# Squared-ReLU attention with an MLP on one Trainium2 core: the first chunk's loads in another order, and v's high part rounded on ScalarE

## The chip, the cores and the metric

The kernel runs on one core of one Trainium2 chip (trn2). The metric is the device time of one execution in microseconds, the median of several runs. A measurement of this kernel can tell about 0.2% (4 us) from no change.

The engines are called as in the profile: PE (matmul), DVE (VectorE), ACT (ScalarE), POOL (GpSimd) and SP (SyncE, which issues most DMAs here). Each engine works through its own instructions in order, and so does each queue of DMA issues: whatever stands behind a waiting instruction waits too.

## The reference

```python
# batch 4, seq S = 3008, d_model 256, d_qk 64, d_ff 2048
scores = (1.0 / S) * np.matmul(z, z.transpose(0, 2, 1))
attn = np.maximum(scores, 0.0) ** 2
out = np.matmul(attn, v)
x = (u * out).reshape(B * S, D)
h = x @ w_in
g = h * np.clip(h + 3.0, 0.0, 6.0) / 6.0
return g @ w_out
```

w_in and w_out come in as 64-bit floats, the rest as 32-bit floats.

## The kernel before, in words

**Tiling.** Each batch has 6 chunks of 512 rows (the last has 448), so there are 24 chunks; in the trace chunks are counted from 0. A chunk is worked through in 12 pairs of two 128-row blocks of keys. For each pair `scores` makes s (four matmuls, z times z), relu and square, and `attend` adds the pair to o (twelve matmuls). The matmuls use a 32-bit format that rounds its operands. So every operand is kept as a high part, rounded, and a low part, the rest: vh and vl, ah and al, zx and zy (each holding a high and a low half), w_in_h and w_in_l. `split` (L75 to L78) makes the two: ACT copies to the high part, which rounds, and DVE subtracts. Each product takes three matmuls.

**Symmetry.** The scores are symmetric. Where block k of chunk c is needed as block c of chunk k later, the square r2 is stored to DRAM (tiles d, `keep`, L257 to L260), fetched again (tiles l, `fetch_pair`, L240, four DMAs a pair), transposed on DVE to rm (`turn`, L271) and split (`from_mirror`, L285, L287). At most two fetched pairs exist at a time; `fetch_mirrored` fetches the next ones, both from the main loop and at the end of each `turn`.

**Weights.** The 64-bit weights are taken apart on DVE in pieces of 128x512: `split64` and `finish64` make 8 DVE steps a piece (L101, L106, L110, L114, L119, L123, then L131, L133) and one ACT cast (L117). There are 16 pieces, in the order in which the MLP reads them: in 0, in 1, out 0, in 2, and so on to in 7, out 6, out 7. `weight_ops` is a generator, and `weight_work(n)` takes n steps of it; its first step issues the loads (wraw) of the first two pieces. wraw tiles come from the pool of tag "r" (5 buffers), the same that holds the relu rt, the square r2 and the transposed rm. `weight_needed` takes steps until the piece that a unit reads is ready.

**Order.** One program order is written by hand in the last part: a few calls ahead of the loop, and then, for each chunk i and pair p, `split_v` and `split_z` of the first batch, `scores` of a pair one or two ahead (two while g = 12 i + p is under FIRST = 28), `fetch_mirrored`, `turn_next`, fetches, `weight_work`, `attend`, and from g = 28 on the MLP units: `up` (h, twelve matmuls, L418, L419) and `down` (y, twelve matmuls), 1.4 a pair on average. Each engine's order follows from that.

**First batch.** z and v of batch 0 are loaded while chunk 0 is worked on. Ahead of the loop stand z 0, v 0, z 1, v 1, the first weight loads and then z 2, v 2, v 3. In the loop v 4 and later ones are fetched four pairs ahead, z 3 to z 5 at pairs 0, 2 and 4, each behind the stores of that pair. For batch 0 the high part of v is a second load of the same v by POOL's queue, which rounds on the way (`rounded=b == 0`), and so are the high parts of z for chunks from 2 on.

**Names.** zraw, vraw and wraw are loads as they arrive; t is scratch of the weights; u is the load of u, multiplied by o on DVE (L388); x is that product and xh, xl its split (L77, L78).

Of the kernel before, what the change touches and what calls it, by code (L numbers as in the profile page):

```python
# [13 lines left out]
B, S, D, DQK, DFF = 4, 3008, 256, 64, 2048  # L14
NT = B * S
P = 128
CH = 512
NCH = 6
NJ = 24
NPAIR = NJ // 2  # L20
# [10 lines left out]
def relu2_attention_then_hswish_mlp(  # L31
# [22 lines left out]
    nc = tc.nc  # L54
# [14 lines left out]
    def f(ap):  # L69
        return ap.bitcast(F32)  # L70
# [4 lines left out]
    def split(hi, lo, raw, rounded=False):  # L75
        if not rounded:
            nc.scalar.copy(out=hi, in_=raw)  # L77
        nc.vector.tensor_tensor(out=lo, in0=raw, in1=f(hi), op=ALU.subtract)  # L78
# [86 lines left out]
    def fetch_v(b, p):  # L165

        if b == 0 and p < NPAIR - 1:
            raw = vpool.tile([P, 2, D], F32, tag="vl", name="vraw")
        else:
            raw = stg.tile([P, 2, D], F32, tag="stg", name="vraw")  # L170
        vh = vpool.tile([P, 2, D], F32R, tag="vh", name="vh")
        vt[b, p] = vh
        raws["v", p] = raw
        j0 = p * 2 * P
        for dst, queue in ((raw, nc.sync), (vh, nc.gpsimd))[:1 if b else 2]:
            if p < NPAIR - 1:
                queue.dma_start(
                    out=dst, in_=v[b, j0:j0 + 2 * P, :].rearrange("(r q) d -> q r d", q=P)
                )
            else:  # L180
                queue.dma_start(out=dst[:, 0, :], in_=v[b, j0:j0 + P, :])
                for h in range(2):
                    queue.dma_start(out=dst[64 * h:64 * h + 64, 1, :], in_=v[b, j0 + P:S, :])

    def split_v(b, p):
        vh, raw = vt[b, p], raws.pop(("v", p))
        vl = vpool.tile([P, 2, D], F32R, tag="vl", name="vl")
        split(vh, vl, raw, rounded=b == 0)
        vt[b, p] = (vh, vl)

    def fetch_z(b, k):
        if b == 0:
            raw = xpool.tile([P, CH], F32, tag=("xh0", "xh1", "xl0", "xl1")[k % 4], name="zraw")
        else:
            raw = stg.tile([P, CH], F32, tag="stg", name="zraw")
        zx = zpool.tile([P, CH], F32R, tag="zx", name="zx")
        zy = zpool.tile([P, CH], F32R, tag="zy", name="zy")
        zt[b, k] = (zx, zy)
        raws["z", k] = raw
        cols = slice(k * CH, (k + 1) * CH)  # L200
        nc.sync.dma_start(out=raw, in_=zz[b, :, cols])
        if b == 0 and k > 1:
            nc.gpsimd.dma_start(out=zx[0:64], in_=zz[b, 0:64, cols])
            nc.gpsimd.dma_start(out=zy[64:128], in_=zz[b, 64:128, cols])
# [149 lines left out]
    def width(c):  # L354
        return CH if c < NCH - 1 else S - CH * (NCH - 1)
# [20 lines left out]
    def load_u(b, c):  # L376
        n = width(c)
        t0 = b * S + c * CH
        t = upool.tile([P, 2, CH], F32, tag="u", name="u")
        nc.sync.dma_start(  # L380
            out=t[:, :, :n], in_=ut[:, t0:t0 + n].rearrange("(k p) t -> p k t", p=P)
        )
        raw_x[b, c] = t
# [69 lines left out]
    chunks = [(b, c) for b in range(B) for c in range(NCH)]  # L453
# [63 lines left out]
    def weight_work(n):  # L517
        for _ in range(n):
            next(w_ops, None)
# [39 lines left out]
    with tc.manual_schedule():  # L559
        nc.vector.memset(three, 3.0)  # L560
        fetch_z(0, 0)
        fetch_v(0, 0)
        split_z(0, 0)
        fetch_z(0, 1)
        fetch_v(0, 1)
        weight_work(1)
        split_v(0, 0)
        split_z(0, 1)
        scores(0, 0, 0)
        fetch_z(0, 2)  # L570
        fetch_v(0, 2)
        scores(0, 0, 1)
        fetch_v(0, 3)
        g_done = 2
        to_fetch += [(b, c, p) for b, c, p in pairs if p // 2 < c]
        g_turned = [2]
        for i, (b, c) in enumerate(chunks):
            ahead = b + 1 if c == NCH - 1 and b + 1 < B else None
            for p in range(NPAIR):
                g = i * NPAIR + p  # L580
                lead = 2 if g < FIRST else 1
                if i == 0:
                    if p + 1 < NPAIR:
                        split_v(0, p + 1)
                    if p % 2 == 0 and p // 2 + 2 < NCH:
                        split_z(0, p // 2 + 2)
                early = lead == 2 and p == NPAIR - 1
                if early:
                    attend(b, c, p)
                while g_done < min(g + lead + 1, len(pairs)):  # L590
                    scores(*pairs[g_done], square_on_act=i < 3)
                    g_done += 1
                if p > 3:
                    fetch_mirrored()
                if p < NPAIR - 1 or early:
                    turn_next()
                if i == 0:
                    if p + 4 < NPAIR:
                        fetch_v(0, p + 4)
                    if p % 2 == 0 and p // 2 + 3 < NCH:  # L600
                        fetch_z(0, p // 2 + 3)
                    if p == 6:
                        load_u(*chunks[0])
                        load_u(*chunks[1])
                maybe_split()
                if g >= FIRST:
                    weight_work(5)
                elif p < NPAIR - 2:
                    weight_work(4 if i else 2)
                if ahead and p < NPAIR - 1:  # L610
                    if p:
                        split_v(ahead, p - 1)
                    if p < NPAIR - 2:
                        fetch_v(ahead, p)
                    if p % 2 == 1:
                        fetch_z(ahead, p // 2)
                    elif p:
                        split_z(ahead, p // 2 - 1)
                elif b and c == 0 and p < 4:
                    if p in (1, 2):  # L620
                        split_v(b, NPAIR - 3 + p)
                    if p < 2:
                        fetch_v(b, NPAIR - 2 + p)
                    if p == 2:
                        fetch_z(b, NCH - 1)
                    if p == 3:
                        split_z(b, NCH - 1)
                if not early:
                    attend(b, c, p)
                    turn_next()  # L630
                if p == NPAIR - 1:
                    avs[0] += 1
                total = len(pairs) - FIRST
                target = max(0, g + 1 - FIRST) * ((len(chunks) - 1) * NU - 4) // total
                mlp_units(target - units_done[0])
        mlp_units(1)
        maybe_split()
        mlp_units(len(chunks) * NU - units_done[0])
# [35 lines left out]
```

## Time and profile before

| | |
|---|---|
| median of 3 runs | 1997.01 us (1996.62 to 1998.65) |
| profiled execution, time | 1998.23 us |
| profiled execution, span | 1996.4 us |
| PE busy | 1959.4 us, 98%, 8688 matmuls |
| DVE busy | 1280.7 us, 64% |
| ACT busy | 987.5 us, 49% |
| DMA queues | 178.14 MB; SP's 34.3% of 16 engines' span, POOL's 0.9% |

The profile is of one execution. Busy time is the sum of the instructions of an engine; matmuls overlap, so a matmul lasts 0.39 us and the next one starts 0.227 us after it. The granted clock of PE is given as a share of its full speed: 1.00 is 2.4 GHz and 0.50 is 1.2 GHz. An "idle before" in a row of the timeline is how long the engine stood still ahead of that row, with what ended it; "issue" stands for a wait that the profile doesn't name.

### The profile page before, as it was taken

What the parts mean: (1) busy time and instruction counts of PE and PEld (TensorE: products, weight loads), DVE (VectorE), ACT (ScalarE), POOL (GpSimd) and SP (SyncE); (2) the same over time, 40 slices, a digit from 0 to 9 for tenths busy, and PEclk for the clock granted to TensorE, in tenths of its full rate; (3) what the DMA queues carried; (4) which work ended last, traced back from release to release, by engine and by line L of the source; (5) the groups of instructions that cost most, each with busy time, mean ns of one, the idle gap of its engine ahead of it and who ended that gap; (6) DMA issues with size and microseconds to landing.
All of it is one profiled execution on the core that took longest, in us unless ns stands there. A gap on an engine that the chain in (4) does not pass through costs nothing.

```text
span 1996.4 us, 22062 instructions
## 1 busy us (share of the span) xinstructions
PE 1959.4 (98%) x8688; PEld 1637.0 (82%) x8688; DVE 1280.7 (64%) x1277; ACT 987.5 (49%) x1057; POOL 14.2 (1%) x26
## 2 busy tenths in 40 slices
PE   7899999999999999999999999999999999999999
PEld 5677788788888888888888888888888888888888
DVE  5798765676556566577565665657756565666654
ACT  6665444455444444456544454444554544444343
POOL 2000000000000000000000000000000000000000
PEclk9899999999999999999999999999999999999999
DMA  9663233424323233253333232324342323332300
GB/s 266 201 160 103 64 82 72 115 71 116 82 64 81 72 74 95 50 128 89 95 82 90 55 93 53 101 62 109 90 116 61 86 59 92 74 82 60 94 10 20
DMA packets 403271, 178.14 MB, mean 89 GB/s; under 512 B 250080, under 2 KB 385248, under 8 KB 403168
## 3 DMA queue, kind: packets, MB, share of 16 engines
q1 hardware_dynamic: 399232, 172.55, 34.3%
q0 software_dynamic: 3936, 4.20, 0.9%
q8 instruction: 68, 1.11, 0.2%
q14 instruction: 35, 0.29, 0.1%
HBM read 104.07 MB, written 72.61 MB: 89 GB/s over the span
## 4 chain that ended last, share of the span: by engine, by line
PE 90%; DVE 4%; DMA 2%; ACT 2%; issue 1%; SPq 1%; DVEq 0%; ACTq 0%
PE o L73 34%; PE h L73 24%; PE y L73 24%; PE s L73 7%; DMA zraw<-in_zz_dram 1%; DVE rm L271 1%; DMA vraw<-in_v_dram 1%; DVE rt L419 1%; DVE al L287 1%; ACT rt L418 0%; ACT gh L77 0%; ACT rt L320 0%; SPq L240 0%; DVE gl L78 0%; DMA d<-r 0%
## 5 line engine op out<-in xcount | busy, mean ns | idle before, releaser
L419 DVE SCALAR_TENSOR_TENSOR rt<-rt,h 128x1024 f32<-128x1024 f32 (+1 forms) x192 | 230.0, 1198 | 420.6 <-ACT rt L418 420.4
L418 ACT ACTIVATE rt<-h,three 128x1024 f32<-128x1024 f32 (+1 forms) x192 | 211.0, 1099 | 550.2 <-PE h L73 544.4
L73 PE MATMUL o<-ah,vl 128*128 128x512 f32 (+1 forms) x1152 | 448.1, 389 | 13.3 <-DVE u L388 6.2
L73 PE MATMUL o<-ah,vh 128*128 128x512 f32 (+1 forms) x1152 | 446.8, 388 | 0.0
L73 PE MATMUL o<-al,vh 128*128 128x512 f32 (+1 forms) x1104 | 429.2, 389 | 3.5 <-DVE al L287 3.5
L73 PE MATMUL y<-gh,w_out_l 128*128 128x512 f32 (+1 forms) x768 | 296.3, 386 | 1.7 <-DVE w_out_l L133 1.7
L73 PE MATMUL y<-gl,w_out_h 128*128 128x512 f32 (+1 forms) x768 | 296.3, 386 | 1.1 <-DVE gl L78 1.1
L73 PE MATMUL y<-gh,w_out_h 128*128 128x512 f32 (+1 forms) x768 | 296.0, 385 | 0.0
L73 PE MATMUL h<-xh,w_in_l 128*128 128x512 f32 (+1 forms) x768 | 295.9, 385 | 0.0
L73 PE MATMUL h<-xl,w_in_h 128*128 128x512 f32 (+1 forms) x768 | 295.9, 385 | 0.0
L73 PE MATMUL h<-xh,w_in_h 128*128 128x512 f32 (+1 forms) x768 | 295.8, 385 | 0.0
L78 DVE TENSOR_TENSOR gl<-rt,gh 128x1024 fp32r<-128x1024 f32 (+1 forms) x192 | 230.7, 1202 | 80.5 <-ACT gh L77 77.9
L73 PEld LDWEIGHTS o<-ah,vl 128*128 128x128 f32 x1152 | 218.2, 189 | 60.6 <-issue 11.9
L77 ACT CAST gh<-rt 128x1024 fp32r<-128x1024 f32 (+1 forms) x192 | 197.2, 1027 | 122.8 <-DVE rt L419 122.8
L73 PEld LDWEIGHTS o<-ah,vh 128*128 128x128 f32 x1152 | 218.3, 189 | 40.9
L73 PEld LDWEIGHTS o<-al,vh 128*128 128x128 f32 x1104 | 209.0, 189 | 45.8 <-DVE al L287 5.7
L320 ACT ACTIVATE rt<-s 128x1024 f32<-128x1024 f32 x168 | 171.3, 1020 | 129.9 <-PE s L73 125.1
L332 DVE TENSOR_TENSOR r<-rt 128x1024 f32<-128x1024 f32 (+1 forms) x140 | 170.0, 1214 | 95.7 <-ACT rt L320 95.6
L340 DVE TENSOR_TENSOR al<-r,ah 128x1024 fp32r<-128x1024 f32 x140 | 171.0, 1221 | 22.3 <-ACT r L330 8.6
L73 PEld LDWEIGHTS y<-gh,w_out_l 128*128 128x128 f32 x768 | 144.2, 188 | 29.8 <-DVE w_out_l L133 1.3
L73 PEld LDWEIGHTS y<-gl,w_out_h 128*128 128x128 f32 x768 | 144.2, 188 | 28.9 <-DVE gl L78 2.1
L73 PEld LDWEIGHTS y<-gh,w_out_h 128*128 128x128 f32 x768 | 144.2, 188 | 27.1
(51 smaller groups left out, 1807.0 us busy)
## 6 DMA issues: line engine op xcount, KB each, us to landing
d<-r SPq DMA_DIRECT2D x220, 256.0 KB, 2.9
l<-d SPq DMA_DIRECT2D x320, 128.0 KB, 3.3
l<-d SPq DMA_DIRECT2D x160, 112.0 KB, 2.9
vraw<-in_v_dram SPq DMA_DIRECT2D x44, 256.0 KB, 3.3
u<-in_ut_dram SPq DMA_DIRECT2D x20, 512.0 KB, 4.2
out_dram<-y SPq DMA_DIRECT2D x40, 256.0 KB, 3.1
zraw<-in_zz_dram SPq DMA_DIRECT2D x24, 256.0 KB, 3.6
wraw<-in_w_in_dram SPq DMA_DIRECT2D x8, 512.0 KB, 4.5
```

What stands on the lines that cost most here:

```text
L73: nc.tensor.matmul(out, lhsT=lhsT, rhs=rhs, start=start, stop=stop)
L77: nc.scalar.copy(out=hi, in_=raw)
L78: nc.vector.tensor_tensor(out=lo, in0=raw, in1=f(hi), op=ALU.subtract)
L271: nc.vector.transpose(out=rn.rearrange("p r (k e) -> p r k e", e=32), in_=t[:, :n // 32].rearrange("p k (r e) -> p r k e", r=2),)
L287: nc.vector.tensor_tensor(out=al[:, :, :n], in0=rn, in1=f(ah[:, :, :n]), op=ALU.subtract)
L320: nc.scalar.activation(out=rn, in_=s[:, :, :n], func=AF.Relu, scale=1.0 / S)
L332: nc.vector.tensor_tensor(out=r2_of, in0=r_of, in1=r_of, op=ALU.mult)
L340: nc.vector.tensor_tensor(out=l_of, in0=r2_of, in1=h_of, op=ALU.subtract)
L418: nc.scalar.activation(out=rn, in_=h, func=AF.Relu, bias=three)
L419: nc.vector.scalar_tensor_tensor(out=rn, in0=rn, scalar=6.0, in1=h, op0=ALU.min, op1=ALU.mult)
```

## The change

Four things change, all of them in the order or the way in which data of the first batch and the weights come in.

- Ahead of the loop z 2, z 3, v 2 and v 3 are fetched before the first score, and the call that issues the first weight loads is gone. In chunk 0, v of four pairs ahead and z 4 and z 5 are fetched at the head of a pair, ahead of its scores and their stores.
- v's high part in batch 0 is made as in other batches, by ACT from the loaded raw tile; POOL's second load of v is gone.
- `fetch_mirrored` is called in the loop only from pair 7 on, where it was from pair 4, and the first two loads of u come at pair 7, where they came at pair 6.
- At pair 0 of every chunk ahead of FIRST no weight steps are taken, so the first weight loads are issued at pair 1 of chunk 0.

```diff
     def split_v(b, p):
         vh, raw = vt[b, p], raws.pop(("v", p))
         vl = vpool.tile([P, 2, D], F32R, tag="vl", name="vl")
-        split(vh, vl, raw, rounded=b == 0)
+        split(vh, vl, raw)
         vt[b, p] = (vh, vl)
...
         split_z(0, 0)
         fetch_z(0, 1)
         fetch_v(0, 1)
-        weight_work(1)
+        fetch_z(0, 2)
+        fetch_z(0, 3)
+        fetch_v(0, 2)
+        fetch_v(0, 3)
         split_v(0, 0)
         split_z(0, 1)
         scores(0, 0, 0)
-        fetch_z(0, 2)
-        fetch_v(0, 2)
         scores(0, 0, 1)
-        fetch_v(0, 3)
...
                 if i == 0:
+                    if p + 4 < NPAIR:
+                        fetch_v(0, p + 4)
+                    if p < 2:
+                        fetch_z(0, p + 4)
                     if p + 1 < NPAIR:
                         split_v(0, p + 1)
...
-                if p > 3:
+                if p > 6:
                     fetch_mirrored()
                 if p < NPAIR - 1 or early:
                     turn_next()
-                if i == 0:
-                    if p + 4 < NPAIR:
-                        fetch_v(0, p + 4)
-                    if p % 2 == 0 and p // 2 + 3 < NCH:
-                        fetch_z(0, p // 2 + 3)
-                    if p == 6:
-                        load_u(*chunks[0])
-                        load_u(*chunks[1])
+                if i == 0 and p == 7:
+                    load_u(*chunks[0])
+                    load_u(*chunks[1])
                 maybe_split()
                 if g >= FIRST:
                     weight_work(5)
-                elif p < NPAIR - 2:
+                elif 0 < p < NPAIR - 2:
                     weight_work(4 if i else 2)
```

In `fetch_v` the loop over two destinations and queues becomes the one load by SP.

**SP, start of chunk 0.** The queue of SP from its first load on; r_181 and r_190 are the square of pair 2, r_226 and r_232 that of pair 3. Before:

```order
L201 DMA zraw<-in_zz_dram 128x512
L177 DMA vraw<-in_v_dram 128x2x256
L201 DMA zraw<-in_zz_dram 128x512
L177 DMA vraw<-in_v_dram 128x2x256
L152 DMA wraw<-in_w_in_dram 128x2x512 x2
L201 DMA zraw<-in_zz_dram 128x512
L177 DMA vraw<-in_v_dram 128x2x256
L177 DMA vraw<-in_v_dram 128x2x256 [waits DMAHW0_49]
L257 DMA d_184<-r_181 512x1x128 [waits DMAHW1_49,Activation_49]
L257 DMA d_184<-r_181 512x1x128 [waits DMAHW2_49]
L177 DMA vraw<-in_v_dram 128x2x256 [waits DMAHW3_49]
L201 DMA zraw<-in_zz_dram 128x512 [waits DMAHW4_49]
```

Now, from the fifth load on (the first four are the same):

```order
L200 DMA zraw<-in_zz_dram 128x512 x2
L176 DMA vraw<-in_v_dram 128x2x256 x2
L176 DMA vraw<-in_v_dram 128x2x256 [waits DMAHW0_49]
L200 DMA zraw<-in_zz_dram 128x512 [waits DMAHW1_49,DVE_49]
L256 DMA d_193<-r_190 512x1x128 [waits DMAHW2_49,Activation_49]
L256 DMA d_193<-r_190 512x1x128 [waits DMAHW3_49]
L176 DMA vraw<-in_v_dram 128x2x256 [waits DMAHW4_49]
L200 DMA zraw<-in_zz_dram 128x512 [waits DMAHW5_49,DVE_49]
L256 DMA d_193<-r_232 512x1x128 [waits DMAHW6_49,Activation_49]
L256 DMA d_193<-r_232 512x1x128 [waits DMAHW7_49]
L152 DMA wraw<-in_w_in_dram 128x2x512 [waits DMAHW0_49,DVE_49]
L152 DMA wraw<-in_w_in_dram 128x2x512 [waits DMAHW1_49]
```

All of z but the last piece stands ahead of the first store now, and the two wraw loads have moved from ahead of the first store to behind the second.

**DVE, pairs 2 to 4 of chunk 0.** The same pairs on DVE, from the al of pair 2 to that of pair 4. Before:

```order
L340 TENSOR_TENSOR al<-r_181,ah 128x1024
L101 TENSOR_SCALAR t_198<-wraw 128x512
L106 SCALAR_TENSOR_TENSOR t_198<-wraw,t_198 128x512
L78 TENSOR_TENSOR vl<-vraw,vh 128x512
L340 TENSOR_TENSOR al<-r_226,ah 128x1024
L110 TENSOR_SCALAR wraw<-wraw 128x512
L114 SCALAR_TENSOR_TENSOR t_198<-wraw,t_198 128x512
L78 TENSOR_TENSOR vl<-vraw,vh 128x512
L78 TENSOR_TENSOR zy<-zraw,zx 64x512
L78 TENSOR_TENSOR zx<-zraw,zy 64x512
L340 TENSOR_TENSOR al<-r_263,ah 128x1024
```

Now:

```order
L339 TENSOR_TENSOR al<-r_190,ah 128x1024 [waits Activation_49]
L78 TENSOR_TENSOR vl<-vraw,vh 128x512 [waits DMAHW6_49,Activation_49]
L339 TENSOR_TENSOR al<-r_232,ah 128x1024 [waits Activation_49]
L101 TENSOR_SCALAR t_242<-wraw 128x512 [waits DMAHW0_49]
L78 TENSOR_TENSOR vl<-vraw,vh 128x512 [waits DMAHW7_49,Activation_49]
L78 TENSOR_TENSOR zy<-zraw,zx 64x512 [waits DMAHW5_49,DMASW2_49]
L78 TENSOR_TENSOR zx<-zraw,zy 64x512 [waits DMASW3_49]
L339 TENSOR_TENSOR al<-r_273,ah 128x1024 [waits PE_49,Activation_49]
```

The first weight step, which waits for its load, stands behind the al of pair 3 and ahead of its vl; it stood a pair earlier.

**DVE, pairs 0 to 2 of chunk 3.** t_1423 and t_1504 are the scratch of the piece in 7, t_1490 and t_1623 that of out 6; the rt is that of the unit that reads in 7. Before:

```order
L131 TENSOR_TENSOR t_1423<-t_1423,w_in_h 128x512
L133 TENSOR_TENSOR w_in_l<-t_1423,w_in_l 128x2x256 [waits DVE_49]
...
L131 TENSOR_TENSOR t_1490<-t_1490,w_out_h 128x512
L133 TENSOR_TENSOR w_out_l<-t_1490,w_out_l 128x512 [waits DVE_49]
L419 SCALAR_TENSOR_TENSOR rt<-rt,h 128x1024 [waits Activation_49]
L78 TENSOR_TENSOR gl<-rt,gh 128x1024 [waits Activation_49]
L287 TENSOR_TENSOR al<-rm,ah 128x1024 [waits Activation_49]
L271 STREAM_TRANSPOSE rm<-l 128x1024 [waits DMAHW2_49,DMAHW7_49,DMAHW1_49,DMAHW0_49]
```

Now:

```order
L131 TENSOR_TENSOR t_1504<-t_1504,w_in_h 128x512
L133 TENSOR_TENSOR w_in_l<-t_1504,w_in_l 128x2x256 [waits DVE_49]
L101 TENSOR_SCALAR t_1657<-wraw 128x512 [waits DMAHW2_49]
L418 SCALAR_TENSOR_TENSOR rt<-rt,h 128x1024 [waits Activation_49]
L78 TENSOR_TENSOR gl<-rt,gh 128x1024 [waits Activation_49]
L286 TENSOR_TENSOR al<-rm,ah 128x1024 [waits Activation_49]
L270 STREAM_TRANSPOSE rm<-l 128x1024 [waits DMAHW6_49,DMAHW7_49,DMAHW1_49,DMAHW0_49]
...
L131 TENSOR_TENSOR t_1623<-t_1623,w_out_h 128x512
L133 TENSOR_TENSOR w_out_l<-t_1623,w_out_l 128x512 [waits DVE_49]
```

The last step of out 6 stood directly ahead of that rt, and stands 12 rows behind it now; the last step of in 7 stands two rows ahead of it, where it stood 13.

## Rows read from the trace of the kernel before

**Rows 1.** The table of stretches (from and to in us, length, then busy time and number of instructions of PE, weight loads, DVE, ACT and POOL, the granted clock of PE, the share of the DMA engines, GB/s).

```profile
0.00:71.10 71.10, 51.86 (x180) 39.48 (x180) 44.28 (x62) 40.82 (x43) 14.23 (x26) 0.88 0.99 258
32.90:38.20 5.30, 5.27 (x13) 4.14 (x14) 3.10 (x5) 5.01 (x6) 0.00 (x0) 0.50 0.51 148
53.90:62.20 8.30, 7.10 (x16) 5.16 (x17) 8.20 (x12) 3.60 (x4) 0.00 (x0) 0.50 1.05 340
72.40:75.90 3.50, 3.50 (x10) 2.77 (x9) 2.79 (x4) 1.04 (x1) 0.00 (x0) 0.52 0.55 110
400.00:1996.00 1596.00, 1589.74 (x7128) 1336.55 (x7126) 994.45 (x938) 773.35 (x829) 0.00 (x0) 1.00 0.31 78
```

**Rows 2.** What PE waited for over the whole span (us in total, times, the longest).

```profile
PE s L73 <- DVE zx L78: 7.1, 2, 6.2
PE s L73 <- issue: 6.9, 2, 4.5
...
PE y L73 <- DVE w_out_l L133: 1.7, 2, 0.9
```

**Rows 3.** The timeline of PE in chunk 0 and where chunk 1 begins (start, duration, operation, idle time before it).

```profile
24.70 0.39 PE L73 MATMUL o<-ah,vl 128*128 128x512 f32 x1
...
29.96 0.47 PE L73 MATMUL s<-zy,zx 128*128 128x512 f32 x1 [2.38 <-issue]
...
41.96 0.39 PE L73 MATMUL s<-zy,zx 128*128 128x512 f32 x1
...
45.58 0.39 PE L73 MATMUL s<-zy,zx 128*128 128x512 f32 x1
...
53.92 0.77 PE L73 MATMUL s<-zy,zx 128*128 128x512 f32 x1 [4.55 <-issue]
...
63.07 0.39 PE L73 MATMUL s<-zx 128*128 128x512 f32 x1
...
71.14 0.47 PE L73 MATMUL o<-ah,vl 128*128 128x512 f32 x1 [2.21 <-DVE vl L78]
```

**Rows 4.** The timelines of SP's queue (start, time of issue, number of issues), of DVE and of ACT in chunk 0.

```profile
18.55 0.63 SPq L201 DMA_DIRECT2D zraw<-in_zz_dram  x1
20.75 1.32 SPq L257 DMA_DIRECT2D d<-r  x2
...
39.26 7.31 SPq L240 DMA_DIRECT2D l<-d  x8
...
47.33 0.47 SPq L201 DMA_DIRECT2D zraw<-in_zz_dram  x1
...
28.46 0.68 DVE L78 TENSOR_TENSOR zy<-zraw,zx 64x512 fp32r<-64x512 f32 x1 [4.81 <-DMA zraw<-in_zz_dram]
...
52.41 0.68 DVE L78 TENSOR_TENSOR zy<-zraw,zx 64x512 fp32r<-64x512 f32 x1 [6.98 <-DMA zraw<-in_zz_dram]
...
19.68 1.04 ACT L330 ACTIVATE r<-rt 128x1024 f32<-128x1024 f32 x1
```

**Rows 5.** The DMA view of three short stretches: the loads of weights issued at 2.6 to 3.7 us, at 53.7 to 54.4 and at 87.9 to 88.6, with their size and the median time to landing in us.

```profile
wraw<-in_w_in_dram SPq DMA_DIRECT2D x2, 512.0 KB, 11.0
...
wraw<-in_w_in_dram SPq DMA_DIRECT2D x1, 512.0 KB, 6.7
...
wraw<-in_w_in_dram SPq DMA_DIRECT2D x1, 512.0 KB, 4.2
```

**Rows 6.** Groups of ACT's instructions from 0 to 74 us, shapes kept apart (count, busy us, mean ns of one, idle time before them and what ended it).

```profile
L320 ACT ACTIVATE rt<-s 128x1024 f32<-128x1024 f32 x12 | 12.3, 1024 | 13.9 <-PE s L73 9.7 <-DMA d<-r 3.8 <-DVE al L340 0.2
L329 ACT ACTIVATE ah<-rt 128x1024 fp32r<-128x1024 f32 x10 | 10.6, 1062 | 0.3
L330 ACT ACTIVATE r<-rt 128x1024 f32<-128x1024 f32 x10 | 10.4, 1045 | 7.8 <-DMA d<-r 7.8
...
L117 ACT CAST w_in_h<-t 128x512 fp32r<-128x512 f32 x2 | 1.2, 598 | 0.0
```

**Rows 7.** The timeline of DVE at the end of chunk 2 and the start of chunk 3.

```profile
181.59 0.69 DVE L344 TENSOR_TENSOR al<-r,ah 128x512 fp32r<-128x512 f32 x1 [1.00 <-ACT r L330]
...
184.20 1.24 DVE L271 STREAM_TRANSPOSE rm<-l 128x1024 f32<-128x1024 f32 x1
185.36 0.39 DVE L119 TENSOR_SCALAR wraw<-t 128x512 uint32<-128x512 uint32 x1
...
188.05 1.22 DVE L287 TENSOR_TENSOR al<-rm,ah 128x1024 fp32r<-128x1024 f32 x1
...
201.56 0.42 DVE L101 TENSOR_SCALAR t<-wraw 128x512 uint32<-128x512 uint32 x1
...
203.08 1.21 DVE L419 SCALAR_TENSOR_TENSOR rt<-rt,h 128x1024 f32<-128x1024 f32 x1
...
207.72 0.65 DVE L114 SCALAR_TENSOR_TENSOR t<-wraw,t 128x512 f32<-128x512 f32 x1
...
210.80 1.21 DVE L419 SCALAR_TENSOR_TENSOR rt<-rt,h 128x1024 f32<-128x1024 f32 x1
...
217.74 0.69 DVE L131 TENSOR_TENSOR t<-t,w_out_h 128x512 f32<-128x512 f32 x1
```

**Rows 8.** The timeline of PE in the same place: the first h of the unit that reads in 7, and the first y of the units that read out 6 and out 7.

```profile
204.59 0.39 PE L73 MATMUL h<-xh,w_in_l 128*128 128x512 f32 x1
...
211.03 0.47 PE L73 MATMUL y<-gh,w_out_l 128*128 128x512 f32 x1 [0.84 <-DVE w_out_l L133]
...
219.20 0.50 PE L73 MATMUL y<-gh,w_out_l 128*128 128x512 f32 x1 [0.89 <-DVE w_out_l L133]
```

More of the change, by code (lines that the diff above doesn't have):

```diff
@@ L174, in fetch_v @@
         j0 = p * 2 * P
[L175 to L183, printed above, removed]
+        if p < NPAIR - 1:
+            nc.sync.dma_start(
+                out=raw, in_=v[b, j0:j0 + 2 * P, :].rearrange("(r q) d -> q r d", q=P)
+            )
+        else:
+            nc.sync.dma_start(out=raw[:, 0, :], in_=v[b, j0:j0 + P, :])
+            for h in range(2):
+                nc.sync.dma_start(out=raw[64 * h:64 * h + 64, 1, :], in_=v[b, j0 + P:S, :])
     def split_v(b, p):
```

## The prediction

> **What bounds the kernel now.** The table of engines comes first: PE is busy 98% of the span, so only the places where PE stands still or runs at its lower clock can be won or lost. The table by stretches says where these are: from 400 us on, PE works 1589.7 of 1596.0 us, all at 1.00; in the first 71.1 us it works only 51.9 us, with a mean granted clock of 0.88 [rows 1]. PE's waits name the causes: s behind the split of z (7.1 us, 6.2 of it the start), s behind "issue" twice (6.9 us in all), and later y behind a weight, w_out_l, 1.7 us [rows 2]. The timeline of PE puts places to them: 2.38 us before the s at 29.96, 4.55 before that at 53.92, 2.21 before the o at 71.14 [rows 3]. For the first two the rows of DVE and SP tell what "issue" hides: DVE waited for zraw until 28.46 and 52.41, and SP had issued those two loads only at 18.55 and 47.33, behind stores, the second also behind 7.31 us of mirrored fetches [rows 4]. A stall costs twice, since the granted clock is lower afterwards: after the second, 8.3 us at 0.50 [rows 1]. In steady state a pair costs PE 3.62 us (the s at 41.96 and at 45.58, 16 matmuls apart, 0.227 each) [rows 3].
>
> So I treat two stages apart: chunk 0, whose loads the change reorders, and the start of the fourth chunk (index 3), some 200 us in, where the weights are first needed and where DVE is the engine that PE waits for.
>
> **Part 1, z and v earlier, chunk 0.** In the new order z2 and z3 and v2 and v3 leave SP before any store, z4 behind them, z5 behind the first store. The waits of DVE for zraw (4.81 and 6.98 us) [rows 4] go, and with them the PE stalls at 29.96 and 53.92.
>
> What is late next is a weight. Before, the two first wraw loads were issued among the first loads and took 11.0 us to land [rows 5], while DVE asked for one only after 18 us. Now they stand in SP's queue behind the store of pair 3, and DVE's order has the first weight step between the al of pair 3 and vl of pair 3. Everything on DVE queues behind that wait. The square that this store writes out starts at 19.68 and takes 1.04, and its two issues start at 20.75 and take 1.32, so the first wraw leaves at 22.1 [rows 4]. Landing took 4.2 us on a quiet queue, 6.7 behind other 512 KB loads, 11.0 in the crowd at the start [rows 5]; here two of them go out together beside one store, and I take 5.5, near the lower two: 27.6. One weight step (0.58, below), vl (0.68, as the split of z [rows 4]) and 0.14 to PE give 29.0 for the o of pair 3, which started at 24.70 before [rows 3]: a new stall of 4.3 us, in place of those removed. Behind it I set one stretch at the low clock, of 2.3 us (13 matmuls in 5.27 us against 2.95 at 0.227 each [rows 1]).
>
> From there PE has six pairs of 3.62 to the end of the last s of the chunk, 21.7 us. From that end (63.07 + 0.23) to the o at 71.14 there were 7.84 us: square, al, transposes, weight steps and vl in DVE's order, which the change leaves as it is [rows 3]. Sum: 4.3 + 2.3 + 21.7 + 7.8 = 36.1 us against 46.4 (24.70 to 71.14): **10.3 us won**. The ends: a landing of 4.2 and no clock stretch give 13.9; a landing of 11.0 gives 4.8.
>
> **Part 2, v rounded on ScalarE.** Twelve loads of v by POOL go. ACT gets 12 casts of 128x512, and the same form on weights took 0.598 us [rows 6], so 7.2 us in chunk 0. Its three passes per pair are 1.02 + 1.06 + 1.05 us [rows 6]; with 0.60 that is 3.7 against PE's 3.62. Casts that stand between pairs thus cost 0 to 0.1 per pair, at most 1.5 us with the weight casts; ACT had 7.8 us of waits for stores of r2 [rows 6], which should become fewer, as wraw takes two of the five r buffers later. I take 0 for both together, and keep 1.5 for the end of the range.
>
> **Part 3, mirrored fetches at p > 6.** The 7.31 us of issues [rows 4] move from pair 4 to pair 7, ahead of the u loads, one weight load and the stores of the last two pairs. Their first transposes come behind the al of the last pair, two pairs (7.2 us) and a square later; the issues end by then. Cover gone would be a wait of 1 us; I take 0.
>
> **Part 4, weights later, which the diff shows in one line.** `elif 0 < p < NPAIR - 2` leaves out the weight steps of pair 0 of every chunk ahead of FIRST: 2 in chunk 0, 4 in chunk 1, 4 in chunk 2, and the call before the loop goes too. DVE is 11 steps behind the old order when the MLP starts, and 5 per pair don't catch up: the order now has the last weights forced in directly ahead of the units that read them. Until the end of chunk 2 each weight still stands well ahead of its unit. In chunk 3 it does not.
>
> I count from the first transpose at the end of chunk 2, at 184.20. There DVE had just waited 1.00 us for ACT, so it cannot have been earlier, and it is not later now [rows 7]. The old order ended w_in's last piece at 201.56, and its h started at 204.59, unhindered [rows 7, 8]. Five weight steps took 2.69 us (185.36 to 188.05) and 3.08 us (207.72 to 210.80) [rows 7], 0.577 each. The new order has 11 steps more ahead of that piece (6.35 us), and also rt, al, gl and a transpose, which stood behind it (203.08 to 207.72, 4.64 us): 201.56 + 6.35 + 4.64 = 212.55. With 0.14 to PE, h can't start before 212.7, 8.1 us later than it did.
>
> Then a chain without overlap. h takes 12 matmuls, 2.72. ACT's relu takes 1.1 with its hop. From rt to behind xl DVE took 210.80 to 217.74, 6.94 us [rows 7], and its order now has those ahead of the rest of the next-to-last w_out piece: 7 steps, 4.04. With 0.14 to PE: 14.9 us, so the y that started at 211.03 starts at 227.6. The last y follows behind another y and o, 5.44 us, at 233.1, where it was 219.20 [rows 8]: **13.9 us lost**. PE stands still for about 8 and 9 us on this way, both longer than the 4.55 that brought the low clock before [rows 1, 3]; I add 2.3 us for each, 4.6. The ends: no such stretch, 13.9; two like that of 53.9 to 62.2 (16 matmuls in 7.10 us against 3.63, 3.5 lost [rows 1]), 20.9.
>
> A rule on that last term. The rows show three stretches at about half clock, with 1.2 to 3.5 us lost in each [rows 1], every one behind a stall of over 2 us [rows 3]. The Trainium skill, in "TensorE: Matmul & The Clock Gate", section "What's actually happening", holds that for modelling "the ramp penalty is <1% of a typical kernel span" and should not be fitted to a count. Without the three new stretches (2.3 + 4.6) the sum would be 1998.3 and not 2005.2: true as a share, and yet all the distance from no change to slower.
>
> **Sum.** -10.3 + 0 + 0 + 13.9 + 4.6 = +8.2 us. The profiled execution took 1998.23 us, its span 1996.4 with 1.8 around it; that is 1.2 above the median of 1997.01, so the profile of the changed kernel should show about 2006.4 and the median 2005.2. The ends of the parts give +0.0 (13.9 won, 13.9 lost) to +17.6 (3.3 won, 20.9 lost).
>
> **Rivals.**
> - *The two sides cancel.* The wraw loads land in 4.2 us, no low clock follows, and the losses in chunk 3 stay near 13.9 to 17: 1997 to 2000. For it: 2.21 us of standstill cost only 1.2 us afterwards [rows 1, 3]. Against: the two long stalls are far longer. Chance 0.17.
> - *The weights don't bind, faster.* The late weights are caught in DVE's slack, and only chunk 0 counts: 1997.0 - 10.3 = 1986.7. For it: y waited for weights only 1.7 us so far [rows 2], so the old order had some room. It decides whether DVE ends w_in's last piece by 204.45; by the order it would have to do 11 steps and four other operations 8 us faster. Chance 0.13.
> - *The early loads don't help, slower still.* The weight loads are as slow as at the start (11.0), and chunk 0 wins 4.8 or less; the change then only swaps zraw for wraw as what DVE waits for. 1997.0 - 4.8 + 18.5 = 2010.7. For it: the same two loads took 11.0 [rows 5]. Against: POOL's loads of v are gone then. Chance 0.08.
>
> **How the numbers follow.** The forecast has the other 0.62: 2005.2, by itself 2001 to 2013. What a measurement can tell from no change is 0.2%, 4.0 us: 1993.0 to 2001.0. The forecast and the third rival are slower: 0.70; the first is the same: 0.17; the second is faster: 0.13. A range from 1994 to 2013 leaves out the second rival and a few hundredths at the top.
>
> **What would show it.** Right: no DVE wait for zraw after 20 us; one for wraw at its first step on weights, near 22 to 28; the chunk's last o on a new pair starting near 61 instead of 71.1; then, ten microseconds earlier than in the old rows, y and h behind L133 for several microseconds twice, near 195 to 220, with a granted clock under 1 there. Wrong: PE without gaps over 2 us between 180 and 240, or the last pair of chunk 0 later than 67.

## The result and the profile after

The changed kernel takes 2020.90 us (median of 4 runs, 2018.25 to 2023.20), the kernel before beside it 1996.82 us. The ratio is 1.0116, 95% interval 1.0103 to 1.0128: slower, as forecast, but by 24 us where 8 were forecast, and outside the range. The profiled execution of the changed kernel has a span of 2021.4 us, 25.0 more than before.

The timeline of PE, with the starts that answer to [rows 3] and [rows 8], and the start of chunk 1's pairs:

```profile
28.53 0.79 PE L73 MATMUL o<-ah,vl 128*128 128x512 f32 x1 [3.94 <-DVE vl L78]
...
68.08 0.80 PE L73 MATMUL o<-ah,vl 128*128 128x512 f32 x1 [8.51 <-DVE vl L78]
...
96.48 0.50 PE L73 MATMUL o<-al,vh 128*128 128x512 f32 x1 [0.98 <-DVE al L339]
...
105.22 0.50 PE L73 MATMUL o<-al,vh 128*128 128x512 f32 x1 [1.19 <-DVE al L339]
...
113.96 0.50 PE L73 MATMUL o<-al,vh 128*128 128x512 f32 x1 [1.70 <-DVE al L339]
...
124.00 0.77 PE L73 MATMUL o<-ah,vl 128*128 128x512 f32 x1 [4.70 <-DVE u L387]
...
197.25 0.47 PE L73 MATMUL o<-ah,vl 128*128 128x512 f32 x1 [1.68 <-DVE u L387]
...
207.74 0.50 PE L73 MATMUL y<-gh,w_out_l 128*128 128x512 f32 x1 [1.46 <-DVE w_out_l L133]
...
217.19 0.77 PE L73 MATMUL h<-xh,w_in_l 128*128 128x512 f32 x1 [6.40 <-DVE w_in_l L133]
...
235.35 0.76 PE L73 MATMUL y<-gh,w_out_l 128*128 128x512 f32 x1 [9.96 <-DVE w_out_l L133]
...
242.88 0.39 PE L73 MATMUL y<-gh,w_out_l 128*128 128x512 f32 x1
```

Two of them in the kernel before:

```profile
120.27 0.69 PE L73 MATMUL o<-ah,vl 128*128 128x512 f32 x1 [3.70 <-DVE u L388]
...
192.99 0.47 PE L73 MATMUL o<-ah,vl 128*128 128x512 f32 x1 [1.49 <-DVE u L388]
```

Read as a ledger, each row against the same matmul before (PE's order is the same in both kernels). The last o of chunk 0, that is the first matmul that adds its last pair: 68.08 for 71.14, **3.1 us won**. The first o behind chunk 1, at 124.00, was at 120.27: 3.7 behind, so **chunk 1 lost 6.8**. Then come the weights: the y at 235.35, which reads out 6, was at 211.03, 24.3 behind; the o at 197.25 was at 192.99 and had been 4.3 behind, so **20.1 were lost there** and 0.5 on the way. The rest of the span adds 0.7: -3.1 + 6.8 + 0.5 + 20.1 + 0.7 = 25.0.

The table of stretches (columns as in [rows 1]) shows that behind 240 us next to nothing is lost:

```profile
190.00:220.00 30.00, 20.15 (x80) 15.32 (x79) 25.72 (x36) 8.69 (x10) 0.00 (x0) 0.93 0.47 105
220.00:240.00 20.00, 10.04 (x31) 7.68 (x30) 13.51 (x17) 5.71 (x7) 0.00 (x0) 0.68 0.30 62
240.00:2021.00 1781.00, 1772.00 (x7928) 1488.65 (x7926) 1104.39 (x1040) 855.98 (x917) 0.00 (x0) 1.00 0.32 78
```

Where chunk 0's gain went is read from DVE and SP (columns as in [rows 4]) and from the DMA view of 56.5 to 60 us (columns as in [rows 5]):

```profile
27.45 0.43 DVE L101 TENSOR_SCALAR t<-wraw 128x512 uint32<-128x512 uint32 x1 [5.69 <-DMA wraw<-in_w_in_dram]
...
65.14 1.25 DVE L270 STREAM_TRANSPOSE rm<-l 128x1024 f32<-128x1024 f32 x1 [6.65 <-DMA d<-r]
```

```profile
50.89 4.83 SPq L239 DMA_DIRECT2D l<-d  x8
55.77 1.00 SPq L379 DMA_DIRECT2D u<-in_ut_dram  x2
56.87 0.41 SPq L152 DMA_DIRECT2D wraw<-in_w_in_dram  x1
57.38 1.21 SPq L256 DMA_DIRECT2D d<-r  x2
```

```profile
d<-r SPq DMA_DIRECT2D x3, 256.0 KB, 7.0
u<-in_ut_dram SPq DMA_DIRECT2D x1, 512.0 KB, 5.9
wraw<-in_w_in_dram SPq DMA_DIRECT2D x1, 512.0 KB, 6.7
```

The first row is the forecast wait for wraw (forecast 27.6 and, for o, 29.0; measured 27.45 and 28.53). The second wasn't foreseen. The first transpose at the end of chunk 0 writes rm into a buffer of the r pool, and what it waited for is the store of a square (d<-r) that holds that buffer. By the times it is the store of pair 10: its square was ready at 53.6 (ACT's last pass over it starts at 52.53 and takes 1.04), but SP was issuing eight mirrored fetches, two u loads and a weight load, and let it go at 57.38. Its second half, issued at about 58.0, lands 7 us later, at 65.0, where rm starts (the store of pair 11, issued from 58.68, would land after that). vl of the last pair stands behind rm on DVE, and PE stood still for 8.51 us.

Chunk 1's new pace, from the timelines of DVE and of ACT:

```profile
89.72 1.22 DVE L339 TENSOR_TENSOR al<-r,ah 128x1024 fp32r<-128x1024 f32 x1
90.86 0.68 DVE L114 SCALAR_TENSOR_TENSOR t<-wraw,t 128x512 f32<-128x512 f32 x1
...
92.65 0.68 DVE L131 TENSOR_TENSOR t<-t,w_out_h 128x512 f32<-128x512 f32 x1
95.20 1.23 DVE L339 TENSOR_TENSOR al<-r,ah 128x1024 fp32r<-128x1024 f32 x1 [1.87 <-ACT r L329]
```

```profile
91.57 0.62 ACT L117 CAST w_in_h<-t 128x512 fp32r<-128x512 f32 x1 [2.20 <-DVE t L114]
92.10 1.03 ACT L319 ACTIVATE rt<-s 128x1024 f32<-128x1024 f32 x1
93.16 1.06 ACT L328 ACTIVATE ah<-rt 128x1024 fp32r<-128x1024 f32 x1
94.12 1.04 ACT L329 ACTIVATE r<-rt 128x1024 f32<-128x1024 f32 x1
```

A ring between two engines that each work in order. L114 makes t, L117 casts it on ACT. Before the change, the groups of four steps between two al were L110, L114, L119, L123 and L131, L133, L101, L106: t is ready ahead of an al, and the cast is queued behind the squares of the next pair. In chunk 1 the steps are now seven late (three from chunk 0 and four from its own pair 0), the group behind an al is L114, L119, L123, L131, and L131 begins `finish64`, which hands waiting casts to ACT ahead of its own subtraction. So the cast stands ahead of the next relu in ACT's queue, while its L114 stands behind an al on DVE. ACT waits 2.20 us for DVE, then relu and both squares follow, and DVE's next al waits 1.87 us for those. Two pairs take 8.74 us (the o at 96.48 and at 105.22) where PE needs 7.25 (32 matmuls, 0.227 each).

### The profile page after: what moved, and what is told of

It reads as the page before. It is cut to its first block, busy times and chain, and to the rows that moved or that the text cites. A ratio compares the mean times of both kernels' runs of the same rounds, so it can differ in the third digit from the quotient of the medians.

```text
span 2021.4 us, 22028 instructions
## 1 busy us (share of the span) xinstructions
PE 1963.7 (97%) x8688; PEld 1640.3 (81%) x8688; DVE 1280.8 (63%) x1277; ACT 992.6 (49%) x1069; POOL 4.4 (0%) x12
## 4 chain that ended last, share of the span: by engine, by line
PE 88%; DVE 5%; ACT 4%; DMA 2%; issue 1%; SPq 0%; DVEq 0%; ACTq 0%
PE o L73 33%; PE h L73 24%; PE y L73 24%; PE s L73 7%; ACT rt L319 1%; DMA zraw<-in_zz_dram 1%; DVE al L339 1%; DVE rt L418 1%; ACT rt L417 1%; DVE al L286 1%; ACT r L329 1%; DVE rm L270 1%; ACT ah L328 0%; DVE gl L78 0%; DMA vraw<-in_v_dram 0%
## 5 line engine op out<-in xcount | busy, mean ns | idle before, releaser
L339 DVE TENSOR_TENSOR al<-r,ah 128x1024 fp32r<-128x1024 f32 x140 | 171.0, 1221 | 32.5 <-ACT r L329 18.7
L73 PEld LDWEIGHTS y<-gh,w_out_l 128*128 128x128 f32 x768 | 145.0, 189 | 39.3 <-issue 10.3
L73 PEld LDWEIGHTS h<-xh,w_in_l 128*128 128x128 f32 x768 | 144.7, 188 | 34.6 <-issue 6.8
L286 DVE TENSOR_TENSOR al<-rm,ah 128x1024 fp32r<-128x1024 f32 (+1 forms) x120 | 141.1, 1176 | 44.9 <-ACT ah L284 44.7
```

Source lines behind the costliest of these rows:

```text
L73: nc.tensor.matmul(out, lhsT=lhsT, rhs=rhs, start=start, stop=stop)
L286: nc.vector.tensor_tensor(out=al[:, :, :n], in0=rn, in1=f(ah[:, :, :n]), op=ALU.subtract)
L339: nc.vector.tensor_tensor(out=l_of, in0=r2_of, in1=h_of, op=ALU.subtract)
```

## Experiments

All kernels are edits of the changed kernel, except where said. Ratios are against the kernel before, run on the same chip (medians 1998.09, 1998.09 and 1998.87 us in the three sets). The steps are called n late where DVE has been given n steps fewer by that place than before the change: in the changed kernel three at the end of chunk 0, seven in chunk 1 and eleven from chunk 2 on.

| kernel | median us | ratio, 95% interval |
|---|---|---|
| changed | 2020.90 | 1.0116 (1.0103 to 1.0128) |
| b_weights | 2025.80 | 1.0136 (1.0119 to 1.0153) |
| w_pair0 | 2013.36 | 1.0075 (1.0060 to 1.0090) |
| w_phase | 2005.40 | 1.0033 (1.0021 to 1.0044) |
| u_p8 | 2018.14 | 1.0101 (1.0086 to 1.0116) |
| w_first | 2005.61 | 1.0037 (1.0024 to 1.0050) |
| mirror_p3 | 2020.28 | 1.0111 (1.0092 to 1.0131) |
| mirror_p8 | 2019.91 | 1.0107 (1.0091 to 1.0122) |
| pool_v | 2022.17 | 1.0119 (1.0104 to 1.0134) |
| best1 | 1988.34 | 0.9949 (0.9934 to 0.9964) |
| best2 | 1980.50 | 0.9910 (0.9893 to 0.9926) |
| best2_m3 | 1985.65 | 0.9936 (0.9919 to 0.9952) |
| best2_pool | 1992.60 | 0.9970 (0.9960 to 0.9980) |

Three questions: is it the number of late weight steps or their place that costs (the first five kernels below), what holds the last pair of chunk 0 (the next three), and what do the parts bring once that is mended (the last four).

**b_weights: the weight part alone.** The kernel before with two edits:

```diff
-        weight_work(1)
...
-                elif p < NPAIR - 2:
+                elif 0 < p < NPAIR - 2:
```

> The kernel before with only the weight part of the change: no call that issues the first weight loads ahead of the loop, no weight steps at pair 0 of chunks 0 to 2. First theory: this part alone gives the loss of chunk 1's pace (6.8) and that of chunk 3 (20), less 0 to 3 us for r buffers that come free in chunk 0: 2022, from 2017 to 2026. Rival: the losses need the moved loads and stores; then under 2008.

Slower by 1.36% (the whole change is slower by 1.16%, with overlapping intervals). Of its waits of PE (columns as in [rows 2]), those for w_out_l, w_in_l and al are those of the changed kernel to 0.1 us:

```profile
PE y L73 <- DVE w_out_l L133: 11.4, 2, 10.0
PE o L73 <- ACT r L330: 8.0, 1, 8.0
...
PE h L73 <- DVE w_in_l L133: 6.4, 1, 6.4
...
PE o L73 <- DVE al L340: 3.9, 3, 1.7
```

So this edit alone brings nearly all of the losses of chunks 1 and 3: 4.8 us in chunk 1, of the 6.8 of the ledger, and 19.2 up to the y of out 6, of its 20.1. The 8.0 us stand in chunk 0, before the o at 33.46, where ACT's relu waits 5.34 us for a store of r2; why that store is late there was not tried.

**w_pair0: eight of the eleven steps back.**

```diff
-                elif 0 < p < NPAIR - 2:
+                elif (i or p) and p < NPAIR - 2:
```

> The changed kernel with the weight steps at pair 0 of chunks 1 and 2 put back (8 of the 11 steps that were left out). First theory: the stalls in front of h and y at 210 to 236 us (6.4 and 10.0 us in the changed kernel) come from these steps alone; three steps stay late, so about 17 of the 20 us lost there return: 2004, from 2001 to 2007, with the al waits of chunk 1 (1.0 to 1.7 us each) as they were. Rival: DVE is late there because of what was lost in chunks 0 and 1, not because of the steps; then the stalls stay and the time is within 4 us of 2020.9.

A miss by 9 us. The waits of h and of the first y go, but one y, at 225.55, still waits 9.57 us for w_out_l: three late steps are enough to put that piece behind the relu of a later unit on DVE. The loss goes by thresholds, not by steps: up to the y of out 6 some 11 of the 20.1 us come back, and not 17. And PE's waits for al stay, 5.1 us in all: three late, as here, and seven late, as in the changed kernel, put the same steps between two al of chunk 1, as the groups have four. Chunk 1 is even some 2.5 us longer than in the changed kernel.

**w_phase: three more steps in chunk 0.**

```diff
-                    weight_work(4 if i else 2)
+                    weight_work(4 if i else 3 if 4 < p < 8 else 2)
```

> The changed kernel with three more weight steps in chunk 0 (one more at each of pairs 5, 6 and 7), so that in chunk 1 the same steps stand between two al as before the change: L110, L114, L119, L123 and then L131, L133, L101, L106. First theory: chunk 1 runs at 4.37 us a pair in the changed kernel because L131 falls into the group of L114, which puts ACT's weight cast ahead of the next relu while it waits for L114; with the old groups it runs at 3.63 a pair again, 6.8 us less, and with three steps fewer to force in chunk 3 some 2 to 4 us less there: 2011, from 2008 to 2014. Rival: chunk 1 is slow because of stores and buffers, and the pace stays over 4.2 us a pair; then the time is 2017 or more.

Better than expected, 15.5 us below the changed kernel. Eight steps are late now from chunk 2 on and four in chunk 1, the groups are the old ones, and no o waits for al (L339) in chunk 1, which takes 48.6 us (49.1 before the change, 55.9 in the changed kernel). The last pair of chunk 0 is mended too, which was not expected of this edit and is luck as far as the theory goes: rm starts at 57.97 without waiting. h and y still wait for L133 (PE's rows, PE's waits, and SP's queue):

```profile
60.91 0.50 PE L73 MATMUL o<-ah,vl 128*128 128x512 f32 x1 [1.98 <-DVE vl L78]
```

```profile
PE y L73 <- DVE w_out_l L133: 9.8, 1, 9.8
...
PE h L73 <- DVE w_in_l L133: 6.2, 1, 6.2
```

```profile
45.74 0.52 SPq L152 DMA_DIRECT2D wraw<-in_w_in_dram  x1
...
56.55 1.21 SPq L256 DMA_DIRECT2D d<-r  x2
```

SP's rows show what else moved. The store of pair 10 still leaves late, at 56.55 (its square was ready at 52.9), and lands at 63.6; rm doesn't wait for it. The weight load that stood directly ahead of that store (56.87 in the changed kernel) leaves at 45.74 now, ahead of the store of pair 9.

60.91 is where the forecast's sum for chunk 0 had put this o (60.8).

**w_first: one step earlier, ahead of the loop.**

```diff
         fetch_v(0, 3)
+        weight_work(1)
```

> The changed kernel with one more weight step ahead of the loop, behind the early z and v loads: the first weight loads leave ahead of every store. This also shifts the weight steps by one, so that the step that makes t (L114) ends a group ahead of al and not begins one behind it. Theory: the wait for wraw at 27.45 and the stall of 3.94 us go (4 to 6 us), and the al waits of chunk 1 go (6.8 us), while the stalls behind L133 near 207 to 235 stay within 1 us of 1.5, 6.4 and 10: 2010 us (2003 to 2013, the last pair of chunk 0 being open by 6 us). Rival (the pace of chunk 1 comes from the number of late steps, not from their phase): al waits stay with ten steps late, 2015 to 2017.

As the theory has it, in all its parts. Ten steps are late from chunk 2 on, six in chunk 1, but L114 now ends a group, ahead of al, and the cast waits 0.5 us or less where it waited 2.20 (the timeline of ACT):

```profile
88.50 0.62 ACT L117 CAST w_out_h<-t 128x512 fp32r<-128x512 f32 x1 [0.39 <-DVE t L114]
```

No o waits for al in chunk 1, which takes 49.7 us. The late waits stay (the timeline of PE), and so does the one at the last pair of chunk 0, 9.25 us:

```profile
61.05 0.80 PE L73 MATMUL o<-ah,vl 128*128 128x512 f32 x1 [9.25 <-DVE vl L78]
...
202.46 0.77 PE L73 MATMUL h<-xh,w_in_l 128*128 128x512 f32 x1 [6.32 <-DVE w_in_l L133]
...
219.85 0.77 PE L73 MATMUL y<-gh,w_out_l 128*128 128x512 f32 x1 [9.98 <-DVE w_out_l L133]
```

In chunk 1, three late have the al waits (w_pair0) and four and six late don't (w_phase, w_first): the place of the steps makes chunk 1's pace, not their number.

**best1: all steps back.** The edits of w_pair0 and w_phase together; from chunk 1 on DVE's order of weight steps is the old one.

> The changed kernel with all its weight steps back: pair 0 of chunks 1 and 2 takes its 4 steps again and pairs 5 to 7 of chunk 0 take 3 instead of 2, so that from chunk 1 on the order of weight steps on DVE is that of the kernel before, lag 0. Theory (the loss is the lag and its phase, nothing else): no wait of al in chunk 1, no wait of h or y for L133 over 2 us near 200 to 240, the last o of chunk 0 near 61 as with three steps added (60.91). From that kernel's 2005.4 the stalls of 6.2 and 9.8 us go and their stretches at the low clock: 1987 us (1984 to 1992), faster than both kernels. Rival (the new order of loads itself makes DVE late in chunk 3): stalls behind L133 stay, over 2000.

17.1 us below w_phase, and faster than the kernel before: with no step late PE waits for w_out_l twice, 0.9 us at the longest, as before the change [rows 2]. The order of loads does not make DVE late in chunk 3; the lag does.

**u_p8: the u loads one pair later,** behind the store of pair 10 (`i == 0 and p == 8`).

> The changed kernel with the first two loads of u at pair 8 of chunk 0 in place of pair 7, so that the store of pair 10 leaves SP ahead of them. First theory: the first transposed tile takes the buffer of r2 of pair 10, and waits 6.65 us for that store, which was issued late and landed beside 1 MB of u; with u behind it the wait falls to 1 to 3 us and the o of the last pair starts 4 to 6 us earlier: 2016, from 2014 to 2018. Rival: the transpose waits for its own fetched tile, whose issues stand where they were; then the wait stays over 5 us and the time is within 2 us of 2020.9.

Moved as expected, a little less: the store left at 54.68, rm waited 4.32 for it instead of 6.65, PE 6.39 instead of 8.51. The store still took 6.2 us to land (60.92). The median fell by 2.8 us, with overlapping intervals.

**mirror_p3: Part 3 alone undone** (`p > 3` again).

> The changed kernel with the mirrored fetches back at pair 4; all else as changed. Theory (the stall of the last pair comes from the eight fetches standing ahead of the store of pair 10): that store leaves SP at about 53.5, lands in 3 to 5 us, rm waits under 1.5 us, the last o of chunk 0 starts near 62 instead of 68.08: 2014.5 us (2012 to 2018). Rival 1 (the store is slow because of the weight and u loads beside it, not because of its place): rm still waits 4 us or more, 2018 to 2021. Rival 2 (the 7 us of issues at pair 4 now delay the stores of pairs 6 and 7 and ACT waits for r buffers): the last o is early but PE stalls near 45 to 50, 2018 or more.

The last pair is eased (rm waits 1.87, PE 2.20), but its o starts at 67.29, hardly earlier, and the median hardly moves. Rival 2 comes nearest, though the last o isn't early: eight fetches at pair 4 hold back stores and v, PE stands still in the middle of the chunk, and the store of pair 10 leaves only at 57.59 (timeline of PE):

```profile
51.60 0.50 PE L73 MATMUL s<-zy,zx 128*128 128x512 f32 x1 [1.20 <-ACT rt L319]
...
56.70 0.80 PE L73 MATMUL o<-ah,vl 128*128 128x512 f32 x1 [3.90 <-DVE vl L78]
...
67.29 0.50 PE L73 MATMUL o<-ah,vl 128*128 128x512 f32 x1 [2.20 <-DVE vl L78]
```

**mirror_p8: the fetches one pair later still** (`p > (6 if i else 7)`).

> The changed kernel with the first mirrored fetches one pair later still (pair 8 of chunk 0), so that the store of pair 10 leaves SP ahead of them. Theory (rm of the last pair waits for that store because the eight fetches and the u loads hold it back in SP's queue): the store leaves at about 53.6 when its square is ready, not at 57.38, the wait of rm falls from 6.65 us to 1 to 3 (then it is the fetch itself that is late), the last o of chunk 0 starts near 63 instead of 68.08: 2016 us (2013 to 2019). Rival (the landing beside the u and weight loads is what counts): the store takes 7 us or more from 53.6, rm starts near 61 to 62 and its fetches are then late as well, 2018 to 2022.

The store left at 51.82, as soon as its square was ready, and no longer holds rm. But the fetch now does, for 5.20 us, since its eight issues took 7.51 us here (SP, then DVE):

```profile
51.82 1.29 SPq L256 DMA_DIRECT2D d<-r  x2
53.16 7.51 SPq L239 DMA_DIRECT2D l<-d  x8
```

```profile
61.91 1.25 DVE L270 STREAM_TRANSPOSE rm<-l 128x1024 f32<-128x1024 f32 x1 [5.20 <-DMA l<-d]
```

The expected o was 63, the measured one 64.85; the gain in the median, 1.0 us, is within the intervals. The wait for the store goes as the theory said, and the fetch's is larger than it said.

**pool_v: Part 2 alone undone.** `split(..., rounded=b == 0)` and POOL's second load of v as in the kernel before.

> The changed kernel with Part 2 alone undone: the high part of v in batch 0 comes by POOL's second load again, ACT has no casts of v. Theory (12 casts of 0.6 us on ACT lie beside PE's work, as predicted at 0): 2020.9 within 3 us, unless the more crowded DMA engines make the first wraw land later, which would add. Rival (the casts stand in ACT's chain of three passes per pair, which leaves no room, 3.7 of 3.62 us): chunk 0 gets up to 7 us shorter, 2014 to 2017.

The same time, out of two effects that cancel. With POOL's loads the first two weight loads take 11.1 us to land (median) instead of 5.9, and PE stands still 9.74 us (DVE, PE, and the DMA view of 20 to 32 us):

```profile
34.63 0.43 DVE L101 TENSOR_SCALAR t<-wraw 128x512 uint32<-128x512 uint32 x1 [11.45 <-DMA wraw<-in_w_in_dram]
```

```profile
35.80 0.76 PE L73 MATMUL o<-ah,vl 128*128 128x512 f32 x1 [9.74 <-DVE vl L78]
...
67.72 0.56 PE L73 MATMUL o<-ah,vl 128*128 128x512 f32 x1 [2.03 <-DVE vl L78]
```

```profile
vh<-in_v_dram POOLq DMA_DIRECT2D x4, 256.0 KB, 7.4
...
wraw<-in_w_in_dram SPq DMA_DIRECT2D x2, 512.0 KB, 11.1
```

In return rm of the last pair starts without a wait, at 64.70, and PE waits 2.03 us there and not 8.51. No wait of PE shorter without ACT's casts is to be seen.

**best2: all steps back, and the first weight loads ahead of every store.** w_first, pair 0 of the later chunks as in w_pair0, and 3 steps at pairs 5 and 6.

> As the kernel with all steps back, but the first weight loads are issued right behind the early z and v loads, ahead of every store, and only pairs 5 and 6 of chunk 0 take 3 steps; lag 0 again. Theory: DVE's wait for wraw at 27.45 (5.69 us) goes, PE's 3.94 us before o at 28.53 too, some 4 to 6 us less than the kernel with all steps back: 1982 us (1979 to 1988). Rival: the two wraw tiles then hold two of the five r buffers from the start, ACT waits for stores of r2 as it did in the kernel before, and the gain is given back: 1987 or more.

The fastest version, 0.9% below the kernel before. The wait for wraw is gone, ACT waits for no store in 10 to 50 us, and the last o of chunk 0 starts at 54.99, 16.1 us earlier than before the change [rows 3]; the span is 17.5 shorter.

**best2_m3 and best2_pool: the fast version with Part 3, and with Part 2, undone.**

> The fast version (all weight steps back, first weight loads ahead of every store; 1980.5) with Part 3 alone undone: mirrored fetches from pair 4 on. Theory (the place of the fetches is bought either way: at pair 4 they hold back the loads of v and the stores in the middle of chunk 0, at pair 7 the last store): with the fetches at pair 4 PE stalls 3 to 5 us near 40 to 50, as it did at 51.60 and 56.70 in the changed kernel with this edit: 1985 us (1982 to 1988). Rival (Part 3 does nothing): 1980.5 within 1.5.

> The fast version (1980.5) with Part 2 alone undone: v's high part by POOL's second load. Theory (the casts cost nothing, but POOL's twelve loads crowd the DMA engines while z and v come in): 1982 us (1979 to 1987). Rival (ACT's casts are on the path in chunk 0): 1975 to 1978.

Part 3 undone costs 5.2 us, as expected: PE waits 3.20 us before the o at 54.02. Part 2 undone costs 12.1 us, more than expected (1992.60 lies outside 1979 to 1987): the first store of r2 lands at 30.0 instead of 20.5 in best2, and ACT stands still (timeline of ACT):

```profile
30.07 1.06 ACT L330 ACTIVATE r<-rt 128x1024 f32<-128x1024 f32 x1 [6.03 <-DMA d<-r]
...
34.80 1.02 ACT L320 ACTIVATE rt<-s 128x1024 f32<-128x1024 f32 x1 [3.67 <-DMA d<-r]
```

## Why the prediction was wrong in size

**Part 1, early loads: right up to the last pair.** The wait for wraw, the o behind it (29.0 forecast, 28.53 measured) and the pace after that held: the last s of the chunk ended at 53.4, for 53.0 in the forecast. w_phase, with the last pair unhindered, has the forecast sum (60.91 for 60.8).

**Part 3: the step that failed first.** "Cover gone would be a wait of 1 us; I take 0" looked at the fetches' own transposes only. The fetches also hold back what stands behind them on SP, and a store that lands late holds its buffer. That is 10.3 forecast and 3.1 won: 7.2 us. The sentence of Part 1 that the 7.84 us up to the last o stay as they are fell with it (they were 14.7), and so came one of the forecast's own signs of being wrong, a last pair later than 67. u_p8 moves the store and rm's wait shrinks to 4.32, mirror_p8 moves it further and the wait for it goes; mirror_p3 shows that the old place isn't free either. The late steps of Part 4 have a share in it: in w_phase and best1 the same fetches stand at pair 7, the store of pair 10 leaves as late, and rm waits for nothing, in best1 although it starts at 57.49, 1.4 us after that store began to be issued. So rm does not need that store's buffer there. In both, the next weight load, whose tile is one of the same pool, leaves SP at about 45.5, ahead of the store of pair 9; that this is what changes rm's buffer is argued, not shown.

**Part 4: the term in the sum was right, a second one was missing; this is the other step that failed.** The forecast lost 13.9 us and 4.6 for the clock, 18.5, up to the last y. That y was at 219.20 [rows 8] and is at 242.88, so 19.4 were lost up to it (20.1 up to the y of out 6). The h that was forecast 8.1 us later than before starts 12.6 later (217.19 for 204.59 [rows 8]); 4.3 of it come from ahead of this stretch, 8.3 from the weights. Three waits make 17.8 of PE's standstill (1.46, 6.40, 9.96), where two made 1.7 before [rows 2]. The clock's part can be read at 0.227 per matmul: 80 matmuls in 20.15 us and 31 in 10.04 make 2.0 + 3.0 = 5.0 for the 4.6; 17.8 - 1.7 + 5.0 = 21.1 is this reading of the 20.1. By themselves these 5.0 us exceed the 4 us that a measurement of this kernel can't tell from no change. As a share of the span they are 0.25%, within what the Trainium skill grants the ramp in "TensorE: Matmul & The Clock Gate", section "What's actually happening" (under 1%).

Missing was what late steps do before they are needed. The prediction asked only whether each weight stands ahead of its unit ("Until the end of chunk 2 each weight still stands well ahead of its unit") and counted steps. It did not ask which steps stand between two al in chunk 1 now. That cost 6.8 us, in a stretch for which the forecast had no term. w_phase, w_first and w_pair0 show that it hangs on the place in the group.

**Part 2: 0 for ACT's casts held**: from 28.5 to 53.4 us of the changed kernel, with the casts on ACT, PE is busy 24.87 of 24.90 us. But taking POOL's loads off the DMA engines, for which the forecast counted nothing, is worth 12.1 us where nothing else holds chunk 0 (best2 against best2_pool), and only lets another wait appear where something does (pool_v).

**Sum:** 8.2 forecast + 7.2 (rm and the store) + 6.8 (casts ahead of relus) + 0.5 (on the way) + 0.9 (Part 4, up to the last y) + 1.3 (behind it) = 24.9, for the 25.0 of the profiles. "Slower" came as forecast, by the mechanism of Part 4. None of the rivals came; none of them had a mechanism at the end of chunk 0 or in chunk 1.

What stays open: how the r buffers are handed out was read from which releaser rm names, not tried with a sixth buffer. Part 1 was not run without Parts 2 and 3 together, so its own share of the 16.1 us that best2 wins in chunk 0 isn't known.

## What to carry to other kernels

When work on one engine is shifted by some steps, look not only at when its results are needed, but at what comes to stand between two neighbours: a cast queued on engine B ahead of B's next critical instruction, while its source stands behind a critical instruction on engine A, makes a ring of two in-order engines and can set the pace of every round. Count in phases (steps modulo a round) as well as in lag, and expect lag to cost by thresholds. Of a block of DMA issues that is moved, list what stands behind it on that queue, and for each store there ask who gets its buffer next.

## What the runs showed of the hardware

- The same eight fetches of 128 KB took SP between 4.63 us (w_phase, at 50.73) and 7.51 us (mirror_p8, at 53.16) to issue, and 7.31 before the change [rows 4].
- The stores of 256 KB issued from 57.38 us of the changed kernel on took 7.0 us from issue to landing, behind 512 KB loads that themselves took 5.9 and 6.7; with POOL's loads of v in flight the 512 KB weight loads took 11.1 us instead of 5.9.
- When PE began again after its waits of 6.40 and 9.96 us, the granted clock was 0.50 (1.2 GHz) from 217.2 to 222.0 and from 235.3 to 238.0 us; over 220 to 240 us it averaged 0.68, and from 240 us on 1.00 (2.4 GHz).
